# Attention and two gated feed-forward stages: a job's sums go back to PSUM and are gated there, with fixed bank roles, other owners for the splits, and buffers on 256-byte multiples

## The chip, the cores and the metric

One core of a Trainium2 chip runs the whole program in one launch. The metric is device microseconds (us) from start to end; a lower number is better. Engines are named as in the profile: PE is TensorE (matrix products), ACT is ScalarE, DVE is VectorE, POOL is GpSimd, SP is SyncE, which issues the transfers. SBUF is the large on-chip memory, PSUM the small one that matrix products write (8 banks here, each 512 float32 columns on 128 partitions).

## The reference

Four sequences of 576 tokens with 8 heads of 64 go through causal attention with a decay; the result, 2304 tokens by 512, goes through two feed-forward stages:

```
scores = q k^T / 8 + cum(log f)_i - cum(log f)_j      # causal
x  = softmax(scores) v                                 # 2304 x 512
h  = x @ w_in;  x = (h * sigmoid(h)) @ w_out           # 512 -> 2048 -> 512
out = ((x @ w_a) * (x @ w_b)) @ w_out2                 # 512 -> 1536 -> 512
```

All of it is held to float32 accuracy.

## The kernel before

**Accuracy by splitting.** A matrix product takes operands rounded to a shorter float format (fp32r). Each operand is therefore split in a high part (ACT copies and rounds it) and a low part (value minus high part, a subtraction on DVE or POOL), and each product is three matmuls: high·high, high·low, low·high.

**Stages.** First 16 pairs of heads go through attention. Then "stage 0": the 2304 tokens are three groups g of 768, the 2048 columns of `w_in` are eight units u of 256; each (u, g) is one job, 24 in all. Then "out 0": blocks of tokens (four of 512, one of 256) times `w_out`, with 16 steps f per block, each of 12 matmuls. Then stage 1 with 36 jobs (u from 0 to 11), and out 1 with 12 steps per block, which writes the result.

**A job** (`job`, L707) is a Strassen-like product: instead of eight block products of 256x384 it makes seven (`PROD`, L683; `product`, L687), each of 6 matmuls of 384 columns. The price is sums. Of a token group `make_forms` (L606) prepares seven forms in a tile `x`: four combinations (`combine`, L617, on tiles `z`) and seven splits (L603 the high part on ACT, L604 the low part on DVE or POOL), each on 128x768 elements. Of a unit of weights `load_unit` (L654) does the like (`w`). The products themselves accumulate in three PSUM banks a, b and g; a is copied by ACT to a tile c at L723 and L731, b at L728, while products go on accumulating in the same bank, and DVE adds the final bank to the copy (L734, L737, L743). So the four results of a job lie partly in c (SBUF), partly in a (PSUM). Stage 0 then gates: h·sigmoid(h) is made as (tanh(h/2)+1)·h with the factor 1/2 folded in later; ACT makes the tanh (L746, L748, L758), and `(t+1)*h` is one DVE instruction of 128x384 (L747, L759, and `gate` L591), or two on POOL (L593, L594). Stage 1 only multiplies (L754, L763). Results go to HBM (`gdram`, `cdram`).

**Out stages.** `out_block` (L780) reads them back per step through a ring of 7 slots, splits them (L794 on ACT, L795 on DVE or POOL, tile `hl`) and multiplies with split weights `wo` (L803). Weights arrive as float64; `decode` (L635) turns a piece of 128x512 into float32 with one ACT instruction, four on DVE (L646, L647, L649, L650) and one POOL addition (L651), and `load_out` (L767) splits it. The first half of the sixteen `wo` pieces of out 0 is asked for during the last jobs, the second half during the first block, each piece behind a ring load that stands `AHEAD` (L777) steps further.

**What sets the order.** All of this is recorded in a plan. Each operation has a priority (a due time), an engine with a fixed cost, and sometimes a second engine (`pool_dve`, L583, and `gate`). A planner turns it into one fixed order per engine and picks the engine. At run time each engine works through its order in sequence and waits by semaphores for what it needs. Tiles share a fixed number of places by tag (`SLOTS`, L261); the four PSUM tags s, t, pv and mm hold 4, 2, 1 and 1 banks. In the kernel before, a bank's tag comes from a cycle of eight (`BANKS`, L702). The lines `make_forms(0, 0, ...)` in the pair loop and `make_forms(0, 1, ...)`, `make_forms(0, 2, ...)` ahead of stage 0 set when the token groups are prepared. The forms of groups 1 and 2 lie in memory that attention uses until its end (`open_late`, L866, marks it "late"), and group 2 holds tokens of the last pair of heads (15), which DVE finishes at L571; so their preparation starts only there.

Of the kernel before, what the change touches and what calls it, by code (L numbers as in the profile page):

```python
# [227 lines left out]
def model_kernel(ctx: ExitStack, tc: tile.TileContext, qk, q0, v, f, w, out):  # L228
# [347 lines left out]

# [77 lines left out]
    def load_unit(stage, n, pr, after=()):  # L654
# [10 lines left out]
        def form(f, k, i):  # L665
            split(k * 2 * P, flat(0, f, k), flat(1, f, k), q(i, k), keys[i:i + k], (wt, f), pr)
# [35 lines left out]
    BANKS = ('s', 's', 's', 's', 't', 'pv', 't', 'mm')  # L702
    turn = cycle(BANKS)

    def bank(name):
        tag = next(turn)
        return buf(mm if tag == "mm" else aps, tag, [P, 512], F32, name)  # L707

    def job(stage, u, g, t):
# [15 lines left out]
        b = bank("b" + name)  # L725
# [265 lines left out]
```

## Time and profile before

| what | value |
|---|---|
| median of 3 runs | 1051.18 us (1049.61 to 1054.39) |
| the profiled execution | 1048.31 us |
| its span, first to last instruction | 1046.6 us |
| mean granted TensorE clock, share of full | 0.989 |
| PE busy | 989.8 us, 95% |
| DVE busy | 697.0 us, 67% |
| ACT busy | 494.4 us, 47% |
| POOL busy | 461.2 us, 44% |
| DMA | 128.40 MB, mean 123 GB/s |

The profiled execution took 1.7 us more than its span; it lies 2.9 us below the median of the runs. Attention fills the span to about 212 us, stage 0 to about 410 us (out 0 begins beside its last jobs), out 0 to about 617 us, stage 1 to about 889 us, and out 1 the rest. A busy share is a mean over these stages, so a stretch view (busy time of each engine in a window) tells more than the page's first part.

### The profile page before, as it was taken

What the parts mean: (1) busy time and instruction counts of PE and PEld (TensorE: products, weight loads), DVE (VectorE), ACT (ScalarE), POOL (GpSimd) and SP (SyncE); (2) the same over time, 40 slices, a digit from 0 to 9 for tenths busy, and PEclk for the clock granted to TensorE, in tenths of its full rate; (3) what the DMA queues carried; (4) which work ended last, traced back from release to release, by engine and by line L of the source; (5) the groups of instructions that cost most, each with busy time, mean ns of one, the idle gap of its engine ahead of it and who ended that gap; (6) DMA issues with size and microseconds to landing.
All of it is one profiled execution on the core that took longest, in us unless ns stands there. A gap on an engine that the chain in (4) does not pass through costs nothing. (4 is left out here: it accounts for less than half of the span.)

```text
span 1046.6 us, 16132 instructions
## 1 busy us (share of the span) xinstructions
PE 989.8 (95%) x5793; PEld 861.4 (82%) x5793; DVE 697.0 (67%) x1249; ACT 494.4 (47%) x1066; POOL 461.2 (44%) x390
## 2 busy tenths in 40 slices
PE   8899989969999999889999998999999999899998
PEld 7565656769999897568888898999999999678888
DVE  7668888497689999997722178676676673932220
ACT  6778888754555554343522263433333332332222
POOL 5627664070276676666400175564444452620003
PEclk9999999989999999999999999999999999999999
DMA  5433444103344468535333102232223325544332
GB/s 145 172 130 111 152 131 125 48 1 152 116 148 145 167 212 306 175 120 174 81 109 85 54 14 86 102 132 95 101 86 114 118 96 196 166 128 134 107 90 86
DMA packets 55983, 128.40 MB, mean 123 GB/s; under 512 B 9436, under 2 KB 13676, under 8 KB 55872
## 3 DMA queue, kind: packets, MB, share of 16 engines
q1 hardware_dynamic: 55792, 126.94, 37.1%
q8 instruction: 45, 0.74, 0.3%
q10 hardware_dynamic: 112, 0.45, 0.2%
q14 instruction: 34, 0.28, 0.1%
HBM read 89.08 MB, written 38.26 MB: 122 GB/s over the span
## 5 line engine op out<-in xcount | busy, mean ns | idle before, releaser
L803 PE MATMUL o<-hl,wo 128*128 128x512 f32 (+1 forms) x1680 | 362.5, 376 | 15.2 <-DVE hl L795 3.4
L803 PEld LDWEIGHTS o<-hl,wo 128*128 128x128 f32 x1680 | 293.8, 189 | 83.1 <-DVE hl L795 5.1
L696 PE MATMUL a<-x,w 128*128 128x384 f32 x1440 | 273.7, 338 | 6.1 <-DVE c L737 2.3
L696 PEld LDWEIGHTS a<-x,w 128*128 128x128 f32 x1440 | 253.4, 189 | 7.9 <-DVE c L737 3.3
L794 ACT CAST hl<-ring 128x512 fp32r<-128x512 f32 (+1 forms) x140 | 80.3, 577 | 186.0 <-PE o L803 169.6
L795 DVE TENSOR_TENSOR hl<-ring,hl 128x512 fp32r<-128x512 f32 (+1 forms) x90 | 72.4, 806 | 136.2 <-ACT hl L794 130.6
L696 PE MATMUL b<-x,w 128*128 128x384 f32 x720 | 146.1, 339 | 10.9 <-ACT c L728 10.0
L795 POOL TENSOR_TENSOR hl<-ring,hl 128x512 fp32r<-128x512 f32 (+1 forms) x50 | 57.6, 1155 | 204.2 <-ACT hl L794 195.0
L696 PEld LDWEIGHTS b<-x,w 128*128 128x128 f32 x720 | 127.2, 189 | 12.4 <-ACT c L728 10.7
L651 POOL TENSOR_TENSOR e<-m,e 128x512 f32<-128x512 f32 x68 | 97.9, 1444 | 75.3 <-DVE e L650 66.9
L604 POOL TENSOR_TENSOR w<-e,w 128x512 fp32r<-128x512 f32 (+1 forms) x39 | 46.1, 1183 | 77.9 <-ACT w L603 51.9
L390 POOL TENSOR_TENSOR qkl<-qk,qkh 128x304 fp32r<-128x304 f32 x60 | 53.9, 931 | 60.2 <-ACT qkh L386 28.1
L696 PE MATMUL g<-x,w 128*128 128x384 f32 x360 | 72.9, 337 | 1.2 <-DVE z L759 0.7
L472 ACT ACTIVATE p<-p,nm 128x512 f32<-128x512 f32 (+3 forms) x128 | 70.7, 558 | 3.1 <-DVE nm L464 3.1
L754 POOL TENSOR_TENSOR z<-c 128x384 f32<-128x384 f32 x29 | 37.0, 1277 | 67.8 <-DVE c L737 67.0
L647 DVE SCALAR_TENSOR_TENSOR m<-raw,m 128x512 uint32<-128x512 uint32 x68 | 66.2, 974 | 0.8
L603 ACT CAST w<-e 128x512 fp32r<-128x512 f32 x80 | 44.3, 566 | 46.9 <-POOL e L671 14.8
L696 PEld LDWEIGHTS g<-x,w 128*128 128x128 f32 x360 | 63.3, 188 | 2.2 <-DVE z L759 1.3
L464 DVE CUSTOM_DVE_ANT_0 p<-s,maskw 128x512 f32<-128x512 f32 (+3 forms) x128 | 55.5, 485 | 13.0 <-PE t_x L514 6.9
L723 ACT COPY c<-a 128x384 f32<-128x384 f32 x60 | 28.7, 478 | 70.5 <-PE a L696 63.7
L650 DVE SCALAR_TENSOR_TENSOR e<-raw,e 128x512 f32<-128x512 uint32 x68 | 60.7, 900 | 0.4
L737 DVE TENSOR_TENSOR c<-a,c 128x384 f32<-128x384 f32 x60 | 33.2, 554 | 35.9 <-PE a L696 35.7
(108 smaller groups left out, 1373.7 us busy)
## 6 DMA issues: line engine op xcount, KB each, us to landing
raw<-in_w SPq DMA_DIRECT2D x68, 512.0 KB
gdram<-z SPq DMA_DIRECT2D x48, 384.0 KB
ring<-gdram SPq DMA_DIRECT2D x64, 256.0 KB
cdram<-z SPq DMA_DIRECT2D x36, 384.0 KB
ring<-cdram SPq DMA_DIRECT2D x48, 256.0 KB
qk<-in_qk SPq DMA_DIRECT2D x15, 608.0 KB
vt<-in_v SPq DMA_DIRECT2D x16, 320.0 KB
rb<-invs SPq DMA_DIRECT2D x32, 128.0 KB
```

The lines of the kernel that those rows point to most:

```text
L390: plan.add("POOL", t_pool(QK // 4), lambda c=c: nc.gpsimd.tensor_sub(lo()[:, c], raw()[:, c], hi().bitcast(F32)[:, c]), [(hi, "h"), raw], ...
L464: plan.add("DVE", t_dve(nj) + 82, lambda out=out, low=low, o=o, mk=mk: nc.vector.tensor_tensor_reduce(out(), o(), mk, -SCALE, 3.0e38, ALU. ...
L472: plan.add("ACT", t_act(sum(IB[ib]), 279), lambda b=b, c=c, nj=sum(IB[ib]): nc.scalar.activation(b()[:, :nj], b()[:, :nj], AF.Exp, bias=nm ...
L603: act(n, lambda: nc.scalar.copy(hi(), val()), reads, [key + (0,)], pr)
L604: pool_dve(n, lambda e: e.tensor_sub(lo(), val(), hi().bitcast(F32)), list(reads) + [key + (0,)], [key + (1,)], pr)
L647: plan.add("DVE", 850, lambda: nc.vector.scalar_tensor_tensor(u(m), high(), 0x80000000, u(m), ALU.bitwise_and, ALU.bitwise_or), [raw], [m] ...
L650: plan.add("DVE", 900, lambda: nc.vector.scalar_tensor_tensor(e(), low(), 2.0 ** -52, e(), ALU.mult, ALU.mult), [raw], ek, pr)
L651: pool(n, lambda g: g.tensor_add(e(), m(), e()), [m], ek, pr)
L696: nc.tensor.matmul(ps()[:, :HB], a, b, start=start and k == 0 and i == 0, stop=k == 1 and i == 2, skip_group_check=not start)
L794: act(n, lambda hl=hl, g=g: nc.scalar.copy(hl()[:, 0], g()), [(ring, i)], [(hl, 0)], p - 6)
L795: pool_dve(n, lambda e, hl=hl, g=g: e.tensor_sub(hl()[:, 1], g(), hl()[:, 0].bitcast(F32)), [(hl, 0), (ring, i)], [(hl, 1)], p - 6)
L803: nc.tensor.matmul(ps[oc]()[:, :n], a, m, start=f == 0 and i == 0, stop=f == nf - 1 and i == 2)
```

## The change

- **Sums back to PSUM (stage 0).** DVE writes the final sum into a PSUM bank, not into c: for b and g in place, for the third sum into a new bank d. ACT takes the tanh from PSUM, four times 384 elements per job (before: once 768, twice 384), and DVE gates four times per job with the PSUM bank as one operand. POOL gates nothing more. Stage 1 writes only d to PSUM, and its product of c and d goes to DVE.
- **Fixed bank roles.** a takes tag s, b takes t, d takes mm, g takes pv; the first two jobs, which begin while attention still runs, take s, s, mm, mm and gate into c. Out blocks alternate between the banks (s, s, s, t) and (s, t, pv, mm).
- **Fixed engines.** The combinations and low parts of x and the low parts `hl` go to DVE alone; those of w and `wo` go to POOL alone. The planner's cost for DVE on SBUF operands goes from 160 + n/0.7 to 100 + n/0.85.
- **Times.** The first token group is prepared later (priority 2·pair+8 for +3), the second and third as well (+2 for -5, +25 for -2), in another order of forms. `AHEAD` goes from 4 to 1. The first unit of stage 1 waits for a late ring load of out 0's first block. Tokens of batch 2 that belong to group 2 are first kept in a buffer `zx`, and two ACT copies bring them to `z` at pair 11.
- **Stores and keys.** The first two jobs store by quarter; a ring load waits only for the halves of a group that it reads.
- **Places.** Two small tiles, `rim` (224 bytes a partition) and `base` (128 bytes), shift what lies behind them, so that the large buffers start on multiples of 256 bytes; before, `hl`, `z`, c, `raw`, m and e started at 224 past such a multiple, x and `wo` at 128.

```diff
+XT = (B - 1) * S - (NG - 1) * GT
+    rim = edge.tile([P, 56], F32, name="rim")
...
+    heads["zx"] = buf(sb, "zx", [P, KC, XT], F32, "zx")
...
     def dve(n, fn, reads, writes, prio, sbuf=False):
-        plan.add("DVE", 160 + n / (0.7 if sbuf else 0.96), lambda: fn(nc.vector), reads, writes, prio)
-
-    def pool_dve(n, fn, reads, writes, prio):
-        plan.add("POOL", 240 + 2.2 * n, lambda: fn(nc.gpsimd), reads, writes, prio,
-                 also=[("DVE", 160 + n / 0.7, lambda: fn(nc.vector))])
+        plan.add("DVE", 100 + n / 0.85 if sbuf else 165 + n / 0.96, lambda: fn(nc.vector), reads, writes, prio)
...
+    def ss(n, fn, reads, writes, prio):
+        dve(n, fn, reads, writes, prio, True)
+
+    def split(n, hi, lo, val, reads, key, pr, eng):
         act(n, lambda: nc.scalar.copy(hi(), val()), reads, [key + (0,)], pr)
-        pool_dve(n, lambda e: e.tensor_sub(lo(), val(), hi().bitcast(F32)), list(reads) + [key + (0,)], [key + (1,)], pr)
+        eng(n, lambda e: e.tensor_sub(lo(), val(), hi().bitcast(F32)), list(reads) + [key + (0,)], [key + (1,)], pr)
...
         form(0, 0)
         combine(1, 3, 1, False)
-        form(5, 1)
         combine(0, 1, 0, True)
-        form(4, 0)
         form(2, 3)
         combine(3, 3, 0, False)
         form(3, 3)
+        form(4, 0)
+        form(5, 1)
...
-    BANKS = ('s', 's', 's', 's', 't', 'pv', 't', 'mm')
-    turn = cycle(BANKS)
...
+        ta, tb, td, tg = ("s", "s", "mm", "mm") if early else ("s", "t", "mm", "pv")
...
+        def gate(i, j, ps, p):
+            k = (0, 1, 1, 2)[2 * i + j]
+            t, key = (lambda: pc(k), (c, k)) if early else (lambda: z()[:, i, j], (z, i, j))
+            act(HB, lambda: nc.scalar.activation(t(), ps()[:, :HB], AF.Tanh, scale=0.5), [ps], [key], p)
+            dve(HB, lambda e: e.scalar_tensor_tensor(t(), t(), 1.0, ps()[:, :HB], ALU.add, ALU.mult), [ps], [key], p)
...
-        dve(HB, lambda e: e.tensor_add(pc(1), pb(), pc(1)), [b], [(c, 1)], at(3) - 3)
+        if stage == 0:
+            z = None if early else zbuf()
+            dve(HB, lambda e: e.tensor_add(pb(), pb(), pc(1)), [(c, 1)], [b], at(3) - 2)
+            gate(0, 1, b, at(3) - 2)
...
-        dve(HB, lambda e: e.tensor_add(pc(2), pa(), pc(2)), [a], [(c, 2)], at(4) - 3)
+        d = bank(td, "d" + name)
+        pd = lambda: d()[:, :HB]
+        dve(HB, lambda e: e.tensor_add(pd(), pa(), pc(2)), [a, (c, 2)], [d], at(4) - 3)
+        if stage == 0:
+            gate(1, 1, d, at(4) - 2)
+        else:
+            z = zbuf()
+            dve(HB, lambda e: e.tensor_mul(z()[:, 1], pc(1), pd()), [(c, 1), d], [(z, 0, 1)], at(4) - 2)
...
-    AHEAD = 4
+    AHEAD, marks = 1, {}
...
-            pool_dve(n, lambda e, hl=hl, g=g: e.tensor_sub(hl()[:, 1], g(), hl()[:, 0].bitcast(F32)), [(hl, 0), (ring, i)], [(hl, 1)], p - 6)
+            ss(n, lambda e, hl=hl, g=g: e.tensor_sub(hl()[:, 1], g(), hl()[:, 0].bitcast(F32)), [(hl, 0), (ring, i)], [(hl, 1)], p - 6)
...
+    sets = cycle((('s', 's', 's', 't'), ('s', 't', 'pv', 'mm')))
...
-            make_forms(0, 0, 0, 2 * pair + 3)
+            make_forms(0, 0, 0, 2 * pair + 8)
...
+        nc.gpsimd.memset(pool.tile([P, 32], F32, name="base")[:, :1], 0.0)
...
-    make_forms(0, 1, 1, 1000 + t - 5)
-    make_forms(0, 2, 2, 1000 + t - 2)
+    make_forms(0, 1, 1, 1000 + t + 2)
+    make_forms(0, 2, 2, 1000 + t + 25)
...
-            load_unit(1, 0, 1000 + t)
+            load_unit(1, 0, 1000 + t, [marks[0, BLOCKS[0][0], F1 - 2]])
```

The order of instructions moves in two places that matter below. The first is VectorE where attention ends and stage 0 begins, from the multiply of the last pair of heads on. A name such as x_0_1 is the forms tile of stage 0, group 1; z0_0_1 and z1_0_1 are the two halves of that group's tokens; c, d, g and a with 0_0_0 belong to job (0, 0) of stage 0. Before:

```order
L571 TENSOR_TENSOR z1_0_2_2401<-pv_15_0_3180,rb_15_3136 128x128
L617 TENSOR_TENSOR z0_0_1_1326<-z1_0_1_1659,z0_0_1_1326 128x2x384
L604 TENSOR_TENSOR x_0_1_3198<-z0_0_1_1326,x_0_1_3198 128x768
L743 TENSOR_TENSOR c0_0_0_3069<-g0_0_0_3202,c0_0_0_3069 128x384
L617 TENSOR_TENSOR z0_0_1_1326<-z0_0_1_1326 128x2x384
L604 TENSOR_TENSOR x_0_1_3198<-z0_0_1_1326,x_0_1_3198 128x768
L617 TENSOR_TENSOR z1_0_1_1659<-z1_0_1_1659,z0_0_1_1326 128x2x384 x2
L604 TENSOR_TENSOR x_0_2_3235<-z1_0_2_2401,x_0_2_3235 128x768
L604 TENSOR_TENSOR x_0_1_3198<-z1_0_1_1659,x_0_1_3198 128x768
L617 TENSOR_TENSOR z0_0_2_2050<-z0_0_2_2050 128x2x384
```

Now, in the same place:

```order
L576 TENSOR_TENSOR z1_0_2_2634<-pv_15_0_3195,rb_15_3139 128x128
L616 TENSOR_TENSOR z0_0_1_1340<-z1_0_1_1684,z0_0_1_1340 128x2x384
L603 TENSOR_TENSOR x_0_1_3215<-z0_0_1_1340,x_0_1_3215 128x768
L603 TENSOR_TENSOR x_0_1_3215<-z1_0_1_1684,x_0_1_3215 128x768
L616 TENSOR_TENSOR z0_0_1_1340<-z0_0_1_1340 128x2x384
L603 TENSOR_TENSOR x_0_1_3215<-z1_0_1_1684,x_0_1_3215 128x768
L603 TENSOR_TENSOR x_0_1_3215<-z0_0_1_1340,x_0_1_3215 128x768
L616 TENSOR_TENSOR z1_0_1_1684<-z1_0_1_1684,z0_0_1_1340 128x2x384 x2
L603 TENSOR_TENSOR x_0_1_3215<-z0_0_1_1340,x_0_1_3215 128x768
L603 TENSOR_TENSOR x_0_1_3215<-z1_0_1_1684,x_0_1_3215 128x768 x2
L769 TENSOR_TENSOR g0_0_0_3201<-g0_0_0_3201,c0_0_0_3072 128x384
```

Before, group 1 and group 2 were prepared interleaved and shared with POOL; now the eleven operations of group 1 stand together on DVE (four combinations at L616, seven low parts at L603), and those of group 2 come later, between the sums and gates of the jobs.

The second place is GpSimd at the start of out 0, where e is a decoded piece, `wo_0_0` and `wo_0_1` the two halves of the split weights and `hl0_0_k` the split of step k of the first block. Before:

```order
L795 TENSOR_TENSOR hl0_0_2_4936<-ring0_4777,hl0_0_2_4936 128x512
L795 TENSOR_TENSOR hl0_0_4_4949<-ring0_4777,hl0_0_4_4949 128x512
L651 TENSOR_TENSOR e_22_4932<-m_22_4794,e_22_4932 128x512
L651 TENSOR_TENSOR e_23_4971<-m_23_4930,e_23_4971 128x512
L604 TENSOR_TENSOR wo_0_0_4518<-e_23_4971,wo_0_0_4518 128x512
L795 TENSOR_TENSOR hl0_0_6_5019<-ring0_4777,hl0_0_6_5019 128x512
L795 TENSOR_TENSOR hl0_0_7_5040<-ring0_4777,hl0_0_7_5040 128x512
L651 TENSOR_TENSOR e_24_5024<-m_24_4998,e_24_5024 128x512
```

Now:

```order
L603 TENSOR_TENSOR wo_0_0_4519<-e_21_4812,wo_0_0_4519 128x512
L650 TENSOR_TENSOR e_22_4910<-m_22_4862,e_22_4910 128x512
L603 TENSOR_TENSOR wo_0_0_4519<-e_22_4910,wo_0_0_4519 128x512
L650 TENSOR_TENSOR e_23_5019<-m_23_4982,e_23_5019 128x512
L603 TENSOR_TENSOR wo_0_0_4519<-e_23_5019,wo_0_0_4519 128x512
L650 TENSOR_TENSOR e_24_5059<-m_24_5022,e_24_5059 128x512
L603 TENSOR_TENSOR wo_0_1_5085<-e_24_5059,wo_0_1_5085 128x512
```

POOL now alternates between the addition of a piece (L650) and its low part (L603); the low parts of `hl`, some of which POOL had, stand on DVE.

## Rows read from the trace of the kernel before

**Rows 1.** The page: span, and busy us, share and instructions of each engine

```profile
span 1046.6 us, 16132 instructions
...
PE 989.8 (95%) x5793; PEld 861.4 (82%) x5793; DVE 697.0 (67%) x1249; ACT 494.4 (47%) x1066; POOL 461.2 (44%) x390
```

**Rows 2.** Busy time by stretch: window, length, engines, clock, DMA

```profile
0.00:196.00 196.00, 176.04 (x1521) 123.00 (x1521) 150.54 (x486) 156.60 (x425) 102.13 (x110) 0.98 0.42 133
212.00:250.00 38.00, 27.61 (x144) 26.98 (x143) 36.10 (x37) 21.39 (x36) 21.31 (x9) 0.87 0.14 52
...
225.00:230.00 5.00, 2.96 (x9) 2.96 (x10) 5.00 (x5) 3.52 (x7) 3.31 (x2) 0.50 0.00 0
...
310.00:350.00 40.00, 36.39 (x202) 34.49 (x201) 39.80 (x55) 21.57 (x43) 28.78 (x25) 1.00 0.41 142
390.00:410.00 20.00, 18.29 (x88) 15.27 (x87) 20.00 (x26) 10.28 (x19) 12.95 (x10) 1.00 0.87 298
410.00:460.00 50.00, 42.27 (x165) 31.09 (x164) 49.35 (x54) 19.15 (x34) 32.50 (x22) 0.97 0.54 172
600.00:640.00 40.00, 35.48 (x243) 34.61 (x242) 31.63 (x26) 20.87 (x40) 29.08 (x22) 1.00 0.04 11
...
880.00:920.00 40.00, 35.09 (x146) 27.58 (x145) 32.34 (x34) 13.51 (x23) 23.41 (x16) 0.96 0.54 175
```

**Rows 3.** The same view of line L803 alone, out-stage matmuls

```profile
390.00:410.00 20.00, 9.78 (x38) 7.08 (x39) 1.00 0.87 298
...
600.00:640.00 40.00, 16.86 (x137) 16.38 (x135) 1.00 0.04 11
...
880.00:920.00 40.00, 31.85 (x125) 24.31 (x126) 0.96 0.54 175
```

**Rows 4.** The chain of waits: start, length, what

```profile
645.81 1.04 PE b L696 x6
...
880.44 2.80 PE o L803 x12
```

**Rows 5.** Timeline of TensorE at the first jobs: start, length

```profile
227.04 2.29 PE L696 MATMUL b<-x,w 128*128 128x384 f32 x6 [8.79 <-ACT c L728]
```

**Rows 6.** Timeline of ScalarE at the same place

```profile
224.91 1.70 ACT L603 CAST x<-z 128x768 fp32r<-128x768 f32 x2 [2.65 <-DVE z L617]
226.52 0.47 ACT L728 COPY c<-b 128x384 f32<-128x384 f32 x1
```

**Rows 7.** Timeline of VectorE at the same place

```profile
211.54 0.82 DVE L571 TENSOR_TENSOR z<-pv,rb 128x448 f32<-128x448 f32 x2 [2.08 <-PE pv L558]
...
225.67 1.81 DVE L604 TENSOR_TENSOR x<-z,x 128x768 fp32r<-128x768 f32 x2
```

**Rows 8.** Single VectorE lines: duration ns min/median/max, first and last start

```profile
L604 DVE TENSOR_TENSOR x<-z,x x23: 946/1460/2601, 118.9 to 636.8; 128x768 fp32r<-128x768 f32 x23
...
L737 DVE TENSOR_TENSOR c<-a,c x60: 542/558/558, 208.9 to 884.3; 128x384 f32<-128x384 f32 x60
...
L759 DVE SCALAR_TENSOR_TENSOR z<-z,a x24: 540/543/555, 236.3 to 409.6; 128x384 f32<-128x384 f32 x24
...
L596 DVE SCALAR_TENSOR_TENSOR z<-z,c x32: 545/559/1652, 238.8 to 401.7; 128x384 f32<-128x384 f32 x32
...
L647 DVE SCALAR_TENSOR_TENSOR m<-raw,m x68: 670/689/1783, 34.5 to 916.3; 128x512 uint32<-128x512 uint32 x68
...
L649 DVE TENSOR_SCALAR e<-m x68: 410/422/1517, 38.4 to 918.0; 128x512 uint32<-128x512 uint32 x68
...
L795 DVE TENSOR_TENSOR hl<-ring,hl x90: 424/693/2046, 393.2 to 1017.7; 128x512 fp32r<-128x512 f32 x87, 128x256 fp32r<-128x256 f32 x3
```

**Rows 9.** Timeline of GpSimd in the first block of out 0

```profile
438.70 1.40 POOL L651 TENSOR_TENSOR e<-m,e 128x512 f32<-128x512 f32 x1 [1.09 <-DVE e L650]
...
443.48 1.41 POOL L651 TENSOR_TENSOR e<-m,e 128x512 f32<-128x512 f32 x1 [1.09 <-DVE e L650]
```

**Rows 10.** Timeline of TensorE at the end, 256 columns

```profile
1029.79 12.87 PE L803 MATMUL o<-hl,wo 128*128 128x256 f32 x106
```

More of the change, by code (lines that the diff above doesn't have):

```diff
@@ L232, in model_kernel @@
     mm = ctx.enter_context(tc.tile_pool(name="mmA", bufs=1, space=PSUM, side="right"))
+    edge = ctx.enter_context(tc.tile_pool(name="edge", bufs=1, side="right"))
+    rim = edge.tile([P, 56], F32, name="rim")
     wp = ctx.enter_context(tc.tile_pool(name="wp", bufs=1, side="right"))
@@ L575, in attend @@
                 t0 = t2
+        if pair == 11:
+            src, keys = heads["zx"], ins.pop((0, NG - 1))
+            ins[0, NG - 1] = []
+            for r, z in enumerate(group(0, NG - 1)):
+                plan.add("ACT", 510, lambda r=r, z=z: nc.scalar.copy(z()[:, :, :XT], src()[:, 2 * r:2 * r + 2]), keys, [(z, "in", "x")], pr + 3)
+                ins[0, NG - 1].append((z, "in", "x"))
     def act(n, fn, reads, writes, prio):
@@ L665, in form @@
         def form(f, k, i):
-            split(k * 2 * P, flat(0, f, k), flat(1, f, k), q(i, k), keys[i:i + k], (wt, f), pr)
+            split(k * 2 * P, flat(0, f, k), flat(1, f, k), q(i, k), keys[i:i + k], (wt, f), pr, pool)
             for j in range(1, k):
@@ L700, in product, with bank, job @@
         plan.add("PE", T_PROD, mms, [key + (i,) for i in range(2)] + [(x, fx, i) for i in range(2)], [ps], pr)
-    BANKS = ('s', 's', 's', 's', 't', 'pv', 't', 'mm')
-    turn = cycle(BANKS)
-    def bank(name):
-        tag = next(turn)
+    def bank(tag, name):
         return buf(mm if tag == "mm" else aps, tag, [P, 512], F32, name)
-    def job(stage, u, g, t):
+    def job(stage, u, g, t, early):
+        ta, tb, td, tg = ("s", "s", "mm", "mm") if early else ("s", "t", "mm", "pv")
         name, step = f"{stage}_{u}_{g}", 2 * T_PROD / 1000
@@ L724, in job @@
         yield at(1)
-        b = bank("b" + name)
+        b = bank(tb, "b" + name)
         pb = lambda: b()[:, :HB]
@@ L753, in job @@
+            gate(0, 0, gm, at(5) - 2)
         else:
-            pool_dve(HB, lambda e: e.tensor_mul(z()[:, 1], pc(1), pc(2)), [(c, 1), (c, 2)], [(z, 1)], last)
+            dve(HB, lambda e: e.tensor_add(pc(0), pg(), pc(0)), [gm], [(c, 0)], at(5) - 2)
         yield at(6)
@@ L783, in out_block @@
         src = (gdram, cdram)[stage]
-        ps = [bank(f"o{stage}_{t0}_{oc}") for oc in range(KC)]
+        ps = [bank(tag, f"o{stage}_{t0}_{oc}") for oc, tag in enumerate(next(sets))]
         for f in range(nf):
@@ L789, in out_block @@
             loaded = plan.dma(480, 4 * P * n, lambda f=f, g=g: nc.sync.dma_start(g(), src[f, :, t0:t0 + n]),
-                     [("g", stage, f, k) for k in range(t0 // GT, (t0 + n - 1) // GT + 1)], [(ring, i)], p - 14)
+                     [("g", stage, f, k // 2, k % 2) for k in range(t0 // HB, (t0 + n - 1) // HB + 1)], [(ring, i)], p - 14)
+            marks[stage, t0, f] = loaded
             if then and AHEAD <= f < AHEAD + nf // 2:
@@ L830, in model_kernel @@
     prepare()
+    plan.add("POOL", 100, lambda: nc.gpsimd.memset(rim[:, :1], 0.0), (), [], -6)
     fill_decays()
@@ L878, in stage_in @@
     def stage_in(stage, nu, seq, hooks, t):
-        gens = {k: job(stage, u, g, t + k * T_JOB) for k, (u, g) in enumerate(seq)}
+        gens = {k: job(stage, u, g, t + k * T_JOB, stage == 0 and k < 2) for k, (u, g) in enumerate(seq)}
         nexts = {k: 1000 + t + k * T_JOB for k in gens}
```

67 lines of the change are left out of this document (29 added, 38 removed).

## The prediction

> **What bounds the kernel now.** I read the page's first part, which shows PE busy for 95% of the span and no other engine above 67% [rows 1]. A kernel so bound can gain only where PE idles or runs slowly, so the second view is busy time by stretch, and in it I looked for stretches in which PE does fewer matmuls than would fit. The yardstick is a dense run in the chain of waits: six matmuls of 384 columns take 1.04 us (0.1733 each), twelve of 512 take 2.80 us (0.2333 each) [rows 4]; 106 of 256 take 12.87 us (0.1214 each) [rows 10]. Count times yardstick, subtracted from the window, is what is lost there [rows 2, 3]:
>
> - 212 to 250 us, start of stage 0: 38 − 144×0.1733 = 13.0
> - 310 to 350, middle of stage 0: 40 − 202×0.1733 = 5.0
> - 390 to 410, end of stage 0: 20 − 38×0.2333 − 50×0.1733 = 2.5
> - 410 to 460, out 0's first block: 50 − 165×0.2333 = 11.5
> - 600 to 640, start of stage 1: 40 − 106×0.1733 − 137×0.1214 = 5.0
> - 880 to 920, start of out 1: 40 − 125×0.2333 − 21×0.1733 = 7.2
>
> Together 44.2 us, in the windows where other work is late for PE; that is what scheduling alone can give back. In each of them DVE is the fullest of the other engines: 36.10 of 38 us, 39.80 of 40, 20.00 of 20, 49.35 of 50, 31.63 of 40, 32.34 of 40 [rows 2]. So the kernel is bound by PE, and where PE waits, by DVE or by what queues behind it.
>
> **The change part by part.** The sum is made against the profiled execution, 1048.3 us.
>
> *Start of stage 0.* PE waits 8.79 us for one ACT copy of bank b [rows 5]. That copy takes 0.47 us and stands behind casts of x that wait for DVE's combinations [rows 6]. DVE is free of attention at about 212.3 us (211.54 + 0.82) [rows 7], and a 128x768 operation on it then takes a median of 1.46 us, up to 2.60, where it can take 0.946 [rows 8]; POOL is busy 21.31 of these 38 us [rows 2]. In the changed order DVE does group 1's eleven operations alone and POOL has no part in x: 11×0.946 = 10.4 us. The last form that the ninth product behind attention needs comes after some ten of them, at 212.3 + 9.5 = 221.8; PE has eight products of 1.04 us from about 211.6 to 219.9. It waits 1.9 us, and about 1 more behind that copy. Group 2's operations are put off beyond the first jobs. The granted clock in 225 to 230 us was 0.50 of full, the lower of its two levels, after the long wait, and 0.87 over the stretch [rows 2]; with a wait this short I let that loss go as well. Loss 13.0 → 3: −10. Bounds: nothing left (−13), or 8 lost (−5) if the first sums and gates queue behind the eleven.
>
> *Middle and end of stage 0.* What DVE will have there: 72 sums at 0.558, 96 gates at 0.543 (L759, the form with a PSUM operand, gates at that price already), 22 operations on x (eleven for each of groups 1 and 2) at 0.946, 16 decoded pieces (two for each of five units, six of `wo`) at 2×(0.689 + 0.422) = 2.22 (L646 is of L649's kind, L650 of L647's) [rows 8]: 40.2 + 52.1 + 20.8 + 35.5 = 148.6 us. PE's 24 jobs of 42 matmuls take 24×42×0.1733 = 174.7 us. DVE has 26 us of slack, where it was full before, and no SBUF-SBUF gate that lasts up to 1.652 us [rows 8]. Loss 7.5 → 1: −6.5. No row shows a DVE instruction that writes PSUM. From one side it costs what the same sum costs now, 0.558; from the other the longest DVE form of that size, 1.652 [rows 8]. I take 0.558, being nearest in operands: it too has a PSUM and an SBUF input. ACT's four tanh from PSUM instead of three instructions are covered, since ACT is busy 21.57 of 40 us [rows 2].
>
> *First block of out 0.* A piece of `wo` there takes POOL from one addition to the next 443.48 − 438.70 = 4.78 us [rows 9], with one addition and one low part on POOL and four decodes and one `hl` on DVE, the very mix that the changed order gives to every piece. In the order 6 of the 16 pieces are split before the block begins, as before. Ten are left: 47.8 us, plus 6 `hl` outside that cycle at 0.693 [rows 8], 4.2, less about 2 for the piece already begun: 50. PE reaches the last step after 15×2.80 + 1.04 = 43 us. Loss 11.5 → 6.5 (7, less the little that the last step overlaps): −5. Bounds: −9 (DVE without waits for POOL), +3 (`hl`, once shared with POOL, late as well: 10 low parts at 0.693 more on a DVE that is full).
>
> *Start of stage 1.* The combinations here move to DVE alone as well, eleven instead of a shared dozen, and POOL keeps silent while DVE does them: 5.0 → 2: −3. Bounds −4.5 and +1.
>
> *Start of out 1.* Six pieces of `wo` late, 6×4.78 + 6×0.693 = 32.8 us, against 11×2.80 = 30.8 of PE: 2 to 3 lost instead of 7.2: −4.2. Bounds −6 and 0.
>
> *Places in memory.* No row shows an effect of a buffer's offset. A 512-column matmul takes 60 ns more than one of 384, which is 0.469 ns a column; between 256 and 384 columns it is 52/128 = 0.405 [rows 4, 10]. If the former were as cheap as the latter, 512 would take 225 ns, 8 less; there are 1344 of that width (1680 at L803 less 28 steps of 12 in the narrow blocks): −10.7. But the 256-column matmuls read the same `hl` places, and carry no such excess, so the offset is not the likely reason. Between 0 and −10 I take −2.
>
> *Attention.* Five more DVE operations of 0.946 (group 0's forms, all on DVE), and two ACT copies for the `zx` buffer; DVE is busy 150.54 of 196 us, ACT 156.60 [rows 2]. Both fit in, though PE's 176.04 is not dense either: +1, from −2 to +5.
>
> The store traffic, the ring keys by half groups, and the two memsets cost nothing that PE waits for: DMA is busy under 0.6 of the time in every stretch with a loss, but for 390 to 410 (0.87) [rows 2], where the keys only let ring loads go earlier.
>
> Sum: −10 − 6.5 − 5 − 3 − 4.2 − 2 + 1 = −29.7, so 1018.6 against the profiled execution, which lies 2.9 us under the median of the runs. Against that median: **1021 us**.
>
> **A rule weighed.** VectorE operations with two SBUF operands run at 0.946 us at best and up to 2.601 beside POOL's, while L759, with one operand in PSUM, never took more than 0.555 [rows 8]. The Trainium skill (SBUF — State Buffer, section "Who interferes with whom") says that VectorE's second SBUF input goes through a port pair shared with GpSimd under an exclusive lock, and that an instruction with at most one SBUF input outside the two-port modes does not contend. By that rule the gates become immune, and the trace agrees (0.555 against 1.652 for L596). The rule speaks against the change in the out stages, where all `hl` are two-SBUF operations on VectorE and all `wo` splits on GpSimd; that result is rival B.
>
> **The rivals.**
>
> A. *The offsets did matter.* The 8 ns go from all 1344 wide matmuls: the sum takes −10.7 where it had −2. 1021 − 9 = 1012. For it: the excess per column is there. Against: the 256-column case.
>
> B. *The pair DVE and POOL stays the bound in the out stages.* If the two exclude each other fully, a piece costs four decodes (2.22), two POOL operations (1.40 for the addition [rows 9], taken for both) and an `hl`: 2.22 + 2.80 + 0.69 = 5.7 us instead of 4.78; ten pieces are 57, and out 0's start loses 57 + 2 − 43 = 16, out 1's 6×5.7 + 4 − 30.8 = 7. So 4.5 and 0 worse than before, 9.5 and 4.2 worse than my sum; with stage 1's start unchanged (3): 1021 + 17 = 1038. For it: DVE was full in these 50 us. Against: the 4.78 us measured is less than 5.7, so they overlap in part.
>
> C. *Writing PSUM from DVE is slow, and DVE becomes the bound of stage 0.* 72 sums stand against 26 us of slack: from 0.558 + 26/72 = 0.92 us each DVE is later than PE. At 1.652 stage 0 needs 72×1.094 = 79 us more DVE time, 53 beyond the slack, and PE waits that long: 1021 + 53 = 1074. It turns slower than before from 0.92 + 30/72 = 1.34 us a sum. For it: no row shows such a write. Against: reads of PSUM at that size show no penalty.
>
> D. *The fixed banks tie PE to DVE's lag.* g and d have one bank each per job of 42×0.1733 = 7.28 us. A bank is held for the product (1.04), the sum (0.558), a tanh (taken as the copy's 0.47 [rows 6]) and the gate (0.543), so about 2.6 us plus handovers. Only when DVE runs more than 4 us late in each job does PE wait; with decode pieces of 2.22 us and x operations in between this occurs at times. If half the jobs lose 2 us, that is 24 us: 1045, no measurable change.
>
> **How the numbers follow.** My forecast 0.54, A 0.17, B 0.15, C 0.05, D 0.09. The likeliest case by itself spans 1010 to 1033 (the bounds of stage 0's start and of out 0 pull by 8 either way). The range that should hold 8 times in 10 goes from 1006 (A with some of the lower bounds) to 1041 (B). What a measurement can tell from no change is 0.5%, about 5.3 us: below 1046 counts as faster. Slower are most of C (0.04), the worse of D (0.02) and B's far end (0.01); the same are a rest of C (0.01), D's middle (0.03) and 0.03 of B: faster 0.86, same 0.07, slower 0.07.
>
> **What would show it.** In the changed profile the stretch from 212 us on should hold about 200 matmuls of 384 columns in 38 us, no wait above 3 us, and a granted clock near 1. L750, L758 and L769 (sums into PSUM) should take 0.54 to 0.60 us; above 0.92 C is right. L718 should never go much over 0.56. L603 for x on DVE should lie at 0.946 in stage 0. The 512-column step should stay at 0.233; 0.225 means A. In out 0's first block the cycle of `wo` pieces on POOL should be near 4.8 us; 5.7 means B. Waits of PE on DVE for banks d or g in most jobs would mean D. The forecast is wrong if the losses of stage 0 only move later, to where group 2's operations now stand between the sums.

## The result and the profile after

The changed kernel takes 1007.28 us (1006.85 to 1007.96), the kernel before 1052.79 beside it: a ratio of 0.957, interval 0.954 to 0.960. The profiled execution took 1007.96, which is 40.4 less than the one before.

First the page: its span, and the busy time of each engine.

```profile
span 1006.2 us, 16196 instructions
...
PE 974.5 (97%) x5793; PEld 859.4 (85%) x5793; DVE 649.2 (65%) x1289; ACT 497.8 (49%) x1092; POOL 361.7 (36%) x336
```

The same number of matmuls now fills 97% of a shorter span. TensorE itself is busy 15.3 us less than in [rows 1], so not all of the gain is idle time; part of the matmuls became shorter. Busy time by stretch, which answers to [rows 2] (columns: window, length, PE, PEld, DVE, ACT, POOL, clock, DMA share, GB/s):

```profile
212.00:250.00 38.00, 37.09 (x218) 35.97 (x215) 34.57 (x55) 23.83 (x45) 0.00 (x0) 1.00 0.19 73
...
310.00:350.00 40.00, 40.00 (x233) 40.00 (x232) 32.36 (x61) 25.59 (x56) 25.25 (x23) 1.00 0.49 174
390.00:410.00 20.00, 19.81 (x88) 16.07 (x86) 19.79 (x23) 9.37 (x16) 11.89 (x8) 1.00 0.72 259
410.00:460.00 50.00, 44.72 (x181) 34.58 (x182) 45.56 (x52) 21.15 (x39) 34.12 (x25) 0.97 0.46 141
590.00:640.00 50.00, 50.00 (x297) 50.00 (x297) 33.13 (x54) 20.81 (x41) 21.23 (x18) 1.00 0.19 69
865.00:900.00 35.00, 32.02 (x138) 25.26 (x137) 23.95 (x29) 12.92 (x23) 13.25 (x9) 1.00 0.44 132
```

Of the 218 matmuls in the first of these stretches 12 still belong to attention; L695, the products of the jobs, has 206 (before, all 144 were such), in the view of [rows 3]:

```profile
212.00:250.00 38.00, 36.53 (x206) 35.61 (x207) 1.00 0.19 73
```

Attention's last matmuls fill the stretch to 212.56 us, and 206×0.1733 = 35.7 us at 384 columns, so 38 − 0.6 − 35.7 = 1.7 us are lost at the start of stage 0. The middle is full, and so are 390 to 410 and the start of stage 1. The granted clock at the first jobs is 1.00 where the stretch had 0.87. What is left stands in 410 to 460 (50 − 181×0.227 = 8.9) and in 865 to 900 (35 − 138×0.227 = 3.7); 0.227 is this kernel's 512-column step, 6.12/27, from a dense piece of its chain of waits:

```profile
499.93 6.12 PE o L818 x27
```

POOL is silent from 212 to 250 us. TensorE's timeline there:

```profile
209.70 2.92 PE L562 MATMUL pv<-th,vt 128*64 128x448 f32 x24
...
222.26 1.16 PE L695 MATMUL b<-x,w 128*128 128x384 f32 x5 [0.91 <-DVE x L603]
```

The wait that was 8.79 us [rows 5] is 0.91, and DVE's last low part of x ends it. TensorE's waits from 205 us to the end (total, times, longest):

```profile
PE o L818 <- ACT wo L602: 4.2, 5, 1.0
PE o L818 <- POOL wo L603: 3.9, 6, 0.9
PE b L695 <- DVE x L603: 0.9, 1, 0.9
PE o L818 <- DVE hl L810: 0.3, 1, 0.3
```

All but one are for `wo` and `hl` in the out stages. Durations of single DVE lines (min/median/max), to be held against [rows 8]:

```profile
L750 DVE TENSOR_TENSOR b<-b,c x24: 551/566/567, 205.4 to 379.8; 128x384 f32<-128x384 f32 x24
...
L718 DVE SCALAR_TENSOR_TENSOR z<-z,g x22: 540/550/555, 232.1 to 383.0; 128x384 f32<-128x384 f32 x22
...
L603 DVE TENSOR_TENSOR x<-z,x x42: 934/952/1597, 119.5 to 603.9; 128x768 fp32r<-128x768 f32 x42
```

A sum written to PSUM takes 0.566 us, a gate from PSUM at most 0.555, and a 128x768 operation a median of 0.952 where it was 1.460. And POOL's additions of `wo` pieces in out 0, two pieces apart:

```profile
411.27 1.67 POOL L650 TENSOR_TENSOR e<-m,e 128x512 f32<-128x512 f32 x1 [1.30 <-DVE e L649]
...
421.18 1.66 POOL L650 TENSOR_TENSOR e<-m,e 128x512 f32<-128x512 f32 x1 [1.29 <-DVE e L649]
```

(421.18 − 411.27)/2 = 4.96 us a piece; it was 4.78 [rows 9].

### The profile page after: what moved, and what is told of

The parts are those of the page before. It is cut to its first block, busy times and chain, and to the rows that moved or that the text cites. A ratio compares the mean times of both kernels' runs of the same rounds, so it can differ in the third digit from the quotient of the medians.

```text
span 1006.2 us, 16196 instructions
## 1 busy us (share of the span) xinstructions
PE 974.5 (97%) x5793; PEld 859.4 (85%) x5793; DVE 649.2 (65%) x1289; ACT 497.8 (49%) x1092; POOL 361.7 (36%) x336
## 4 chain that ended last, share of the span: by engine, by line
PE 84%; DVE 5%; ACT 4%; issue 4%; DMA 1%; SPq 1%; POOL 0%; DVEq 0%; ACTq 0%
PE o L818 29%; PE a L695 24%; PE b L695 12%; PE g L695 6%; PE s L442 4%; PE pv L562 3%; PE t_y L518 2%; PE t_x L518 2%; ACT th L523 2%; ACT p L476 1%; DVE hl L810 1%; DMA rb<-invs 1%; DVE p L468 1%; PE idle L293 1%; PE idle L857 1%
## 5 line engine op out<-in xcount | busy, mean ns | idle before, releaser
L818 PE MATMUL o<-hl,wo 128*128 128x512 f32 (+1 forms) x1680 | 350.8, 370 | 8.4 <-ACT wo L602 4.2
L695 PE MATMUL a<-x,w 128*128 128x384 f32 x1440 | 270.6, 334 | 0.0
L695 PEld LDWEIGHTS a<-x,w 128*128 128x128 f32 x1440 | 251.1, 188 | 0.7 <-DVE d L758 0.3
L810 DVE TENSOR_TENSOR hl<-ring,hl 128x512 fp32r<-128x512 f32 (+1 forms) x140 | 110.9, 793 | 150.8 <-ACT hl L809 147.0
L603 POOL TENSOR_TENSOR w<-e,w 128x512 fp32r<-128x512 f32 x80 | 100.9, 1271 | 269.9 <-ACT w L602 269.6
L650 POOL TENSOR_TENSOR e<-m,e 128x512 f32<-128x512 f32 x68 | 97.5, 1440 | 158.9 <-DVE e L649 132.1
L695 PE MATMUL b<-x,w 128*128 128x384 f32 x720 | 144.4, 335 | 0.9 <-DVE x L603 0.9
L695 PEld LDWEIGHTS b<-x,w 128*128 128x128 f32 x720 | 126.2, 188 | 1.2 <-DVE x L603 1.2
L695 PE MATMUL g<-x,w 128*128 128x384 f32 x360 | 72.2, 334 | 0.0
L695 PEld LDWEIGHTS g<-x,w 128*128 128x128 f32 x360 | 63.2, 188 | 0.2 <-issue 0.2
L737 ACT COPY c<-a 128x384 f32<-128x384 f32 x60 | 28.8, 481 | 68.4 <-PE a L695 51.5
L646 DVE SCALAR_TENSOR_TENSOR m<-raw,m 128x512 uint32<-128x512 uint32 x68 | 60.0, 884 | 0.6
L758 DVE TENSOR_TENSOR d<-a,c 128x384 f32<-128x384 f32 x60 | 33.8, 563 | 37.7 <-PE a L695 37.5
L745 ACT COPY c<-a 128x384 f32<-128x384 f32 x60 | 28.9, 482 | 55.6 <-PE a L695 55.5
L742 ACT COPY c<-b 128x384 f32<-128x384 f32 x60 | 29.0, 483 | 49.8 <-PE b L695 49.4
L649 DVE SCALAR_TENSOR_TENSOR e<-raw,e 128x512 f32<-128x512 uint32 x68 | 52.8, 788 | 0.3
```

What stands on the lines that cost most here:

```text
L603: eng(n, lambda e: e.tensor_sub(lo(), val(), hi().bitcast(F32)), list(reads) + [key + (0,)], [key + (1,)], pr)
L646: plan.add("DVE", 850, lambda: nc.vector.scalar_tensor_tensor(u(m), high(), 0x80000000, u(m), ALU.bitwise_and, ALU.bitwise_or), [raw], [m] ...
L649: plan.add("DVE", 900, lambda: nc.vector.scalar_tensor_tensor(e(), low(), 2.0 ** -52, e(), ALU.mult, ALU.mult), [raw], ek, pr)
L650: pool(n, lambda g: g.tensor_add(e(), m(), e()), [m], ek, pr)
L695: nc.tensor.matmul(ps()[:, :HB], a, b, start=start and k == 0 and i == 0, stop=k == 1 and i == 2, skip_group_check=not start)
L810: ss(n, lambda e, hl=hl, g=g: e.tensor_sub(hl()[:, 1], g(), hl()[:, 0].bitcast(F32)), [(hl, 0), (ring, i)], [(hl, 1)], p - 6)
```

## The experiments

Each kernel ran beside the kernel before, which had 1050 to 1052 us in these runs.

**Places in memory.** Five kernels change only where buffers start. The first leaves out both small tiles:

```diff
-    rim = edge.tile([P, 56], F32, name="rim")
...
-        nc.gpsimd.memset(pool.tile([P, 32], F32, name="base")[:, :1], 0.0)
```

> The changed kernel without the two small tiles rim and base, so that hl, z, c, m, e, raw start at 224 past a multiple of 256 bytes again and x and wo at 128; the order of instructions is the changed one. Theory 'places': the 512-column step of the out stages goes from 0.227 back to 0.232 to 0.237 us, 1344 of them by some 6 ns = 8 to 9 us: 1015.5 us, idle of PE as in the changed kernel. Rival 'order': the shorter step has another reason (less going on beside it), the time stays at 1007 and the step at 0.227.

Measured: 1015.74 us (ratio 0.967, 0.964 to 0.971). The second puts both tiles into the kernel before, and nothing else:

> The kernel before with the two small tiles, and nothing else of the change. 'Places': the 512-column step falls to 0.227 us in dense stretches and the time by 8 to 9 us, to 1044; the idle stretches of PE stay (8.8 us at 218, 11 us in out 0). 'Order': it stays at 1053. If the places also matter to operations on VectorE and GpSimd, the idle stretches shrink as well and it falls below 1040.

Measured: 1043.25 us against 1050.05 (0.992, 0.989 to 0.996). 'Places' holds in both runs. The next two leave out one tile each:

> The changed kernel without base alone: hl, the moving operand of the out stages, starts at a multiple of 256, while wo, their weights, and x start at 128 past one. If the moving operand's place counts: 1007 and a step of 0.227. If that of the weights counts: 1015.5 and 0.233. If both count in part: between.

> The changed kernel without rim alone: hl starts at 224 past a multiple of 256, wo and x at 0. If the moving operand's place counts: 1015.5 and a step of 0.232 to 0.237 in the out stages. If that of the weights counts: 1007 and 0.227.

Measured: 1020.04 (0.971, 0.967 to 0.975) and 1019.55 (0.970, 0.967 to 0.974). Both expectations failed: each of the two is slower than the kernel without any tile. So neither operand's place decides alone, and the next asks for their relation:

```diff
-    rim = edge.tile([P, 56], F32, name="rim")
...
-        nc.gpsimd.memset(pool.tile([P, 32], F32, name="base")[:, :1], 0.0)
+        nc.gpsimd.memset(pool.tile([P, 24], F32, name="base")[:, :1], 0.0)
```

> The changed kernel with rim left out and base cut to 24 columns, so that hl, w, x, wo, ring, z, c, m, e and raw all start at 224 past a multiple of 256 bytes: all alike, but none on a multiple. Theory 'like places': what counts is that a matmul's moving operand and its weights have the same remainder; 1007 us, steps of 0.227 and 0.173. Rival 'multiples': each start has to be a multiple of 256 (or 128); at least the 1015.7 of the kernel without both tiles, or more.

Measured: 1006.94 us (0.957, 0.954 to 0.960), as fast as the changed kernel. Two stretches that are dense in all of them, 470 to 550 us (512 columns) and 650 to 840 (384 columns); the count behind PE's busy time is what to compare. The changed kernel:

```profile
470.00:550.00 80.00, 80.00 (x355) 66.24 (x354) 34.09 (x46) 29.00 (x51) 2.40 (x2) 1.00 0.38 107
650.00:840.00 190.00, 190.00 (x1098) 190.00 (x1097) 118.30 (x209) 68.06 (x132) 93.86 (x85) 1.00 0.30 104
```

Without both tiles:

```profile
470.00:550.00 80.00, 80.00 (x344) 64.38 (x343) 34.88 (x46) 28.04 (x50) 2.58 (x2) 1.00 0.36 106
650.00:840.00 190.00, 190.00 (x1095) 190.00 (x1094) 119.76 (x210) 69.85 (x135) 97.82 (x90) 1.00 0.31 108
```

Without `base`, and without `rim`:

```profile
470.00:550.00 80.00, 80.00 (x346) 64.87 (x345) 35.01 (x46) 28.19 (x50) 2.74 (x2) 1.00 0.36 107
650.00:840.00 190.00, 190.00 (x1084) 190.00 (x1083) 118.75 (x209) 68.86 (x134) 97.64 (x90) 1.00 0.30 106
```

```profile
470.00:550.00 80.00, 80.00 (x345) 64.41 (x344) 36.33 (x49) 28.60 (x50) 3.09 (x2) 1.00 0.37 109
650.00:840.00 190.00, 190.00 (x1083) 190.00 (x1083) 118.72 (x209) 69.40 (x135) 98.28 (x90) 1.00 0.31 109
```

All starts 224 past a multiple of 256:

```profile
470.00:550.00 80.00, 80.00 (x354) 66.24 (x353) 32.83 (x45) 28.45 (x50) 1.10 (x1) 1.00 0.35 100
650.00:840.00 190.00, 190.00 (x1098) 190.00 (x1097) 117.04 (x206) 67.71 (x131) 91.72 (x84) 1.00 0.30 106
```

The kernel before with both tiles:

```profile
470.00:550.00 80.00, 80.00 (x355) 66.11 (x354) 48.18 (x54) 32.71 (x58) 28.38 (x20) 1.00 0.42 125
650.00:840.00 190.00, 190.00 (x1098) 190.00 (x1097) 125.44 (x217) 67.76 (x134) 88.36 (x77) 1.00 0.30 104
```

The weights of the units lie in three places in turn, A, B and C (units 0, 1, 2, then 3, 4, 5, and so on). A and B lie behind `rim`, C lies behind `base` like x, so that in unit C x and w have like remainders in every one of these kernels. The times are means over all units.

| kernel | hl, wo (start modulo 256) | us per 512-column matmul | x, w in units A/B (modulo 256) | us per 384-column matmul |
|---|---|---|---|---|
| changed | 0, 0 | 80/355 = 0.225 | 0, 0 | 190/1098 = 0.1730 |
| all at 224 | 224, 224 | 0.226 | 224, 224 | 0.1730 |
| before, with tiles | 0, 0 | 0.225 | 0, 0 | 0.1730 |
| without tiles | 224, 128 | 0.233 | 128, 224 | 0.1735 |
| without base | 0, 128 | 0.231 | 128, 0 | 0.1753 |
| without rim | 224, 0 | 0.232 | 0, 224 | 0.1754 |

The windows cut a few matmuls at their edges; the chain of the changed kernel, 27 matmuls in 6.12 us, gives 0.227. In the three kernels where a matmul's moving operand and its weights have the same remainder throughout, be it 0 or 224, all steps are short; in the three with some unlike ones the 512-column matmul takes about 6 ns more, and the 384-column one up to 2.4 on the mean. So with both tiles missing 1344×6 ns = 8 us and 2520×0.5 ns = 1.3 us go (8.5 measured by the medians, nearer 11 by the ratios to the kernel before), and with only one missing another 2520×1.8 ns = 4.5 (4.1 on the mean of the two). Multiples of 256 are not needed: how the starts lie to each other decides.

Single jobs show that the rule is less simple for 384 columns. One job is 42 matmuls, from one product into bank b to the like product of the next job. Without `base` (x at 128 throughout), first unit C (w at 128), then a product of unit C between products of unit A, then unit A (w at 0):

```profile
709.12 1.20 PE L695 MATMUL b<-x,w 128*128 128x384 f32 x6
...
716.40 1.20 PE L695 MATMUL b<-x,w 128*128 128x384 f32 x6
...
724.78 1.23 PE L695 MATMUL g<-x,w 128*128 128x384 f32 x6
725.84 2.28 PE L695 MATMUL a<-x,w 128*128 128x384 f32 x12
727.96 1.22 PE L695 MATMUL b<-x,w 128*128 128x384 f32 x6
...
735.35 1.22 PE L695 MATMUL b<-x,w 128*128 128x384 f32 x6
```

Without both tiles, unit A (x at 128, w at 224):

```profile
730.35 1.20 PE L694 MATMUL b<-x,w 128*128 128x384 f32 x6
...
737.63 1.20 PE L694 MATMUL b<-x,w 128*128 128x384 f32 x6
```

Without `base`, unit C among its like takes (716.40 − 709.12)/42 = 0.1733 a matmul and unit A (735.35 − 727.96)/42 = 0.1760, in one and the same kernel. But the product of unit C at 724.78, with like starts, takes 1.06 us for six (0.177), and unit A without both tiles, with unlike starts, takes 7.28/42 = 0.1733. So a matmul's own two starts do not settle its time: what the matmuls beside it read seems to count as well, and some unlike pairs cost nothing at 384 columns. Which relation it is, why it costs time, and whether other moduli would show it too, was not tried.

**Engines of the splits.** The planner may again choose POOL or DVE for combinations and low parts:

```diff
-        dve(n, fn, reads, writes, prio, True)
+        plan.add("POOL", 240 + 2.2 * n, lambda: fn(nc.gpsimd), reads, writes, prio,
+                 also=[("DVE", 160 + n / 0.7, lambda: fn(nc.vector))])
```

(that is the helper for x and `hl`; w and `wo` go through it too.)

> The changed kernel in which the planner again chooses POOL or DVE for each combination and each low part of x, w, wo and hl, at the old costs; PSUM gates, banks, times and places stay as changed. Theory 'shared work lengthens DVE': operations of 128x768 on DVE beside POOL go from 0.95 to about 1.4 us, PE's wait at 218 us comes back in part, as does the loss in out 0 and stage 1: 1016 to 1026 us. Rival 'gates alone': with gates from PSUM DVE has room enough, and the choice of engine costs under 4 us: below 1011.

Measured: 1026.57 us (0.975, 0.972 to 0.978), 19 more than the changed kernel. Its stretches, and DVE's line for the low parts of x:

```profile
212.00:250.00 38.00, 32.55 (x176) 30.64 (x173) 32.66 (x38) 21.16 (x39) 25.38 (x11) 0.91 0.18 68
410.00:460.00 50.00, 41.24 (x164) 31.06 (x163) 47.10 (x48) 21.49 (x38) 34.62 (x26) 0.97 0.48 164
```

```profile
L604 DVE TENSOR_TENSOR x<-z,x x21: 893/1206/2600, 119.6 to 620.0; 128x768 fp32r<-128x768 f32 x21
```

Low parts on DVE take up to 2.6 us again. At the start of stage 0 attention's last product ends only at 213.5 us and 156 of the 176 matmuls are of 384 columns, so 38 − 1.5 − 156×0.1733 = 9.5 us are lost; PE's longest wait there is 3.6 us for a low part of x. Out 0 loses 50 − 164×0.227 = 12.8. The first theory holds, a little above its range.

**Gates.** The sums go to c again and are gated from there, on DVE, all but in the first two jobs:

```diff
-            dve(HB, lambda e: e.tensor_add(pb(), pb(), pc(1)), [(c, 1)], [b], at(3) - 2)
-            gate(0, 1, b, at(3) - 2)
+            dve(HB, lambda e: e.tensor_add(pc(1), pb(), pc(1)), [b], [(c, 1)], at(3) - 2)
+            gate(0, 1, b, at(3) - 2, 1)
...
```

The last argument of `gate` names the part of c to read; the sums of banks d and g are changed likewise.

> The changed kernel with the sums of stage 0 written to c again (but for the first two jobs) and gated from c, on DVE as in the changed kernel, so 66 gates have two SBUF operands. Theory 'port': gates that meet a POOL operation go from 0.55 to as much as 1.65 us; if half of them do, 33 times 1.1 = 36 us more of DVE against 26 us of slack, PE idles again between 310 and 410 us: 1010 to 1018 us. Rival 'only the engine': keeping x and w apart and the gates off POOL is all that counts, 1007 to 1009 us.

Measured: 1010.32 us (1007.63 to 1011.47; 0.960, 0.957 to 0.963), an interval that overlaps that of the changed kernel. The gates from c, and two stretches:

```profile
L719 DVE SCALAR_TENSOR_TENSOR z<-z,c x66: 541/557/1645, 228.1 to 387.2; 128x384 f32<-128x384 f32 x66
```

```profile
310.00:350.00 40.00, 38.69 (x224) 38.33 (x223) 38.87 (x60) 24.74 (x54) 27.04 (x22) 1.00 0.47 172
370.00:390.00 20.00, 17.73 (x93) 16.12 (x92) 17.64 (x29) 10.96 (x22) 7.97 (x5) 1.00 0.93 327
```

Some gates take up to 1.645 us, DVE is at 38.87 of 40, and PE loses 1.2 us at 310 to 350, in one wait for a sum on DVE. The 2.3 us at 370 to 390 are waits for `hl` (1.6 us for ACT's part, 0.6 for DVE's), which no line ties to the gates. So the mechanism is there and the size is small: some 3 us at most, about what the runs can tell. With x and w kept apart on two engines and no gate on POOL, few collisions are left.

**Times of the token groups.** The three old priorities:

```diff
-            make_forms(0, 0, 0, 2 * pair + 8)
+            make_forms(0, 0, 0, 2 * pair + 3)
-    make_forms(0, 1, 1, 1000 + t + 2)
-    make_forms(0, 2, 2, 1000 + t + 25)
+    make_forms(0, 1, 1, 1000 + t - 5)
+    make_forms(0, 2, 2, 1000 + t - 2)
```

> The changed kernel with the old priorities of the three token groups: group 2's eleven operations stand directly behind group 1's on DVE, ahead of the first jobs' sums and gates. Theory 'queue': the first sum into PSUM at 223 us is put off by 11 times 0.95 = 10.4 us, PE waits for a bank and loses 6 to 10 us there: 1013 to 1017 us. Rival 'banks suffice': PE has enough products ahead, below 1010 us.

Measured: 1028.52 us (0.977, 0.974 to 0.981), 21 more. TensorE and then VectorE at the first jobs:

```profile
217.56 2.92 PE L562 MATMUL pv<-th,vt 128*64 128x448 f32 x24
...
241.75 5.49 PE L695 MATMUL a<-x,w 128*128 128x384 f32 x18 [8.14 <-DVE c L718]
```

```profile
240.69 0.56 DVE L769 TENSOR_TENSOR g<-g,c 128x384 f32<-128x384 f32 x1
```

Group 2's operations end only at 240.7, the first sum follows, and PE waits 8.14 us: the first theory's stall. But the last product of attention starts at 217.56, not 209.70: another 8 us are lost earlier. For that, the old priority of the first group alone:

> The changed kernel with the old priority of the first token group alone (group 2 stays put off). Theory 'two costs': of the 21 us that the three old priorities cost, some 8 lie in attention, where group 0's operations, all on DVE, stand too early: 1014 to 1016 us, and the first jobs as in the changed kernel. Rival 'one cost': group 2 alone is at fault, 1007 us.

Measured: 1017.35 us (0.968, 0.966 to 0.971), and the same product starts late as well:

```profile
218.39 2.92 PE L562 MATMUL pv<-th,vt 128*64 128x448 f32 x24
```

So two costs, as the first theory has it, a little above its range: 10 us from group 0's early operations, which now all stand on DVE (8.7 of them by the start of that product, 218.39 − 209.70), and 11 from group 2's. How the early operations make attention longer was not followed step by step.

**AHEAD.**

```diff
-    AHEAD, marks = 1, {}
+    AHEAD, marks = 4, {}
```

> The changed kernel with AHEAD back at 4, so each late piece of wo is asked for behind a ring load three steps further. Theory 'decode-bound': the pieces come at the pace of their decoding (4.8 us each) and not of their loads, the time stays at 1007 to 1008 us. Rival 'loads late': the first late pieces wait for their data, the loss in out 0 and out 1 grows by 3 to 5 us: 1010 to 1012.

Measured: 1008.08 us (1006.49 to 1009.45; 0.960, 0.958 to 0.962): no difference that these runs can tell, as the first theory has it. Late loads are thus not what holds the pieces up; that their decoding does is argued, not tried.

**What is left in the out stages.** First the pieces of `wo` due earlier, then their low parts on DVE as well:

```diff
-    hooks[7, 1] = [lambda p=1000 + end(0) - 10: ...
+    hooks[7, 1] = [lambda p=1000 + end(0) - 30: ...
-    hooks[11, 1] = [lambda p=1000 + end(0) - 10: ...
+    hooks[11, 1] = [lambda p=1000 + end(0) - 25: ...
```

> The changed kernel with the first half of the wo pieces due 30 us (out 0) and 25 us (out 1) before the stage ends, not 10. Theory 'late start': two more pieces are split before out 0 begins, its loss falls from 8 to about 4 us, out 1's from 4 to 2: 1001 to 1003 us. Rival 'full DVE': the pieces push sums and gates of the last jobs back, what is won in out 0 is lost before it: 1006 to 1009 us.

Measured: 1008.64 us (0.961, 0.959 to 0.964). PE's wait in 340 to 410 us, three additions on POOL, the outer ones two pieces apart, and two `hl` on DVE:

```profile
PE g L695 <- DVE z L718: 3.0, 1, 3.0
```

```profile
420.99 1.67 POOL L650 TENSOR_TENSOR e<-m,e 128x512 f32<-128x512 f32 x1 [1.30 <-DVE e L649]
...
425.92 1.40 POOL L650 TENSOR_TENSOR e<-m,e 128x512 f32<-128x512 f32 x1 [1.23 <-DVE e L649]
...
430.90 1.66 POOL L650 TENSOR_TENSOR e<-m,e 128x512 f32<-128x512 f32 x1 [1.30 <-DVE e L649]
```

```profile
426.09 1.77 DVE L810 TENSOR_TENSOR hl<-ring,hl 128x512 fp32r<-128x512 f32 x1
...
430.74 0.68 DVE L810 TENSOR_TENSOR hl<-ring,hl 128x512 fp32r<-128x512 f32 x1
```

The rival is right: the last jobs' gates come 3.0 us late. The pieces still take (430.90 − 420.99)/2 = 4.96 us. The same `hl` operation takes 1.77 us where a POOL addition is already running (425.92 to 427.32) and 0.68 where it starts 0.16 us ahead of one; then the addition takes 1.66 us, not 1.40.

The second kernel keeps these due times:

```diff
-            split(PIECE, ..., (t, f), p, pool)
+            split(PIECE, ..., (t, f), p, ss)
```

> The same, and the low parts of wo on DVE in place of POOL (0.69 against 1.30 us each). Theory 'exclusion': where two-operand operations of DVE and POOL exclude each other, a piece with its hl costs 2.2 + 0.7 on DVE and 1.4 + 1.3 on POOL, 5.6 us in sum, and 5.0 with the low part on DVE; the cycle of pieces falls below 4.5 us and the time below that of wo_early30 by 1 to 3 us. Rival 'DVE alone': DVE, already full there, gets 0.7 us more per piece, cycle 5 us or more, and 1 to 4 us more than wo_early30.

Measured: 1004.10 us (1001.12 to 1004.42; 0.956, 0.953 to 0.958). Its additions on POOL two pieces apart:

```profile
419.05 1.34 POOL L650 TENSOR_TENSOR e<-m,e 128x512 f32<-128x512 f32 x1 [2.96 <-DVE e L649]
...
427.65 1.60 POOL L650 TENSOR_TENSOR e<-m,e 128x512 f32<-128x512 f32 x1 [2.96 <-DVE e L649]
```

4.30 us a piece: the exclusion theory, though its own sum for a piece was 5.0. The kernel beats the two other kernels with which it shared a chip, wo_early30 and ahead4, by 4 us; against the changed kernel's own ratio, 0.9569, its 0.9556 lies within the interval. It is thus the fastest of the study by median, but not shown to beat the changed kernel.

The fixed bank roles, the buffer `zx`, the stores by quarter and the later load of stage 1's first unit were not undone by any run; what they are worth by themselves is not shown.

## Why the prediction was right

- Direction and range held: 1021 us forecast, 1006 to 1041, measured 1007.28, at the low edge. It lies below the 1010 to 1033 of the likeliest case, and inside the range only because that was stretched to rival A. On the profiled executions −29.7 was forecast and −40.4 came; the terms below, as measured, add up to −37.5, and the other 2.9 are not traced.
- *Start of stage 0* (−10): the loss of 13.0 went to 1.7, with one wait of 0.91 us, which a low part of x ends at 222.26 us, where 221.8 was forecast; −11.3. Without POOL in x the operations took 0.952. The undone engines and the undone times each bring back 7 us or more here.
- *Middle and end of stage 0* (−6.5): 7.5 went to nothing. A sum written to PSUM took 0.566, next to the lower bound, so rival C is out. D is out too: PE waits for no bank in the view of waits. That the gates read PSUM is not what most of this rests on: gated from c again, the kernel loses some 3 us at most, and with the engines undone instead, 310 to 350 us still holds 233 matmuls. What both kernels keep is that no gate runs on POOL; no run undid that, or both parts at once.
- *Start of stage 1* (−3): 5.0 went to nothing.
- *First block of out 0* (−5) and *out 1* (−4.2): 11.5 went to 8.9 and 7.2 to 3.7. The first is mis-sized by 2.4: I took 4.78 us a piece, as if the changed order gave each piece the mix of [rows 9], and it became 4.96. The mix is another: the cycle of [rows 9] held one `hl` on DVE (0.68 us), the two pieces from 411.27 to 421.18 hold three, 1.77 us each. That these make the difference is argued from the times only. Rival B's mechanism is at work, at a fifth of the step to its 5.7 us. The Trainium skill's rule (SBUF — State Buffer, section "Who interferes with whom") is borne out by the 1.77 against 0.68 us of one operation, and by wo_mix's shorter cycle.
- *Places in memory* (−2): measured 8.5 (nearer 11 by the ratios), and 6.8 in the kernel before; rival A's mechanism. This is the step that was sized worst. The reasoning was that the 256-column matmuls read the same `hl` and carried no excess; they carry none in any of the kernels, with like or unlike starts (none over 0.122), so they proved nothing. And the cause is not each start by itself, as the term had it, but how the starts lie to each other; 1.3 us of it lie with the 384-column matmuls, which the term left out.
- *Attention* (+1): DVE's multiply of the last pair starts at 212.45 against 211.54 [rows 7]: +0.9, no more than such kernels differ among themselves (211.26 in the one with `AHEAD` at 4). That it stays so depends on the later priority of group 0, which the prediction had not priced; without it attention takes some 9 us longer.

## What to carry to other kernels

A cheap operation that is late can be worth more than a dear one: keeping each kind of two-operand work on one engine of the pair DVE and POOL, and the urgent group alone on it, gave back most of TensorE's idle time here: undoing the owners cost 19 us, undoing the times 21. Not only two-operand work is held up: in the kernel before, L649 on DVE, with one operand, took 0.422 us in the median and 1.517 at most [rows 8], and 1.49 at 441.18, beside a low part on POOL that ran from 440.84 to 442.39. When an operation moves to one engine, its priority has to move with it. And step times per column, compared between shapes, point at a cost of placement; the control for it has to be a shape that can show it.

## What was not expected

How the starts of a matmul's SBUF operands lie to each other changes the matmuls' times: with like remainders modulo 256 in the whole kernel, 0.227 us for 512 columns and 0.173 for 384; with differences of 32, 96 or 128 bytes, 0.231 to 0.233 for 512 and, on the mean, 0.1735 to 0.1754 for 384; nothing for 256. It is not the pair of one matmul alone: a unit with like starts took 0.1733 among its like and 0.177 between products of another unit, and one with unlike starts (128 and 224) took 0.1733. Correcting one of two operands alone made the kernel slower (1020 us) than correcting neither (1015.7).
